# Four blocks' transposes moved from DMA to TensorE, three attention steps and a rescaling placed later, one output buffer fewer

## The chip, the cores and the metric

The kernel runs on one core of a Trainium2 chip. A core has TensorE (PE, matmuls), VectorE (DVE), ScalarE (ACT), GpSimd (POOL) and SyncE (SP), each with its own instruction queue, and 16 DMA engines that all queues share. The metric is the device time of one execution in microseconds (us); the lower the better.

## What is computed

Sliding-window attention with sink tokens, and behind it an RMS norm and a gated feed-forward network (SwiGLU), for 4 sequences of 768 tokens, 8 heads of 64:

```python
scores = scale * np.matmul(q, k.transpose(0, 1, 3, 2))
is_sink = pos[None, :] < n_sink                    # n_sink = 4
in_window = (rel >= 0) & (rel < window)            # window = 128
a = softmax(np.where(is_sink | in_window, scores, -1e9))
x = matmul(a, v)                                   # 3072 tokens x 512
xn = x / sqrt(mean(x * x) + 1e-6) * rms_g
g = xn @ w_gate                                    # 512 -> 1536
out = (g * sigmoid(g) * (xn @ w_val)) @ w_out      # 1536 -> 512
```

## The kernel before

The 3072 tokens are 24 blocks of 128, six to a sequence (`NT`), and four blocks make a group: six groups of 512 tokens (`GB`, `NG`). A block passes through these steps:

- `load_q`, `load_k`, `load_v` (L105 to L124): POOL issues the loads, which convert to bf16. `L.g` in a list of work is all three for block g.
- `T.g` (`a_T`, L298): q and k of a block are transposed into `qkT`, by PE for blocks below `DMA_T_FROM` = 11 and by DMA transposes on SP's queue (L309) from there on.
- `S.g` (`a_S`, L442): scores of block g's keys against its own queries and those of the next block (L455), the exponential on ACT (L465), and the causal masks, on POOL (L431, L436) or DVE (L429).
- `ss` and `a.g`: scores and values of the four sink tokens (L367, L497), for two blocks at a time.
- `v.g.u` (L504): attention times values on PE (L516, L520), reciprocal and norm on DVE (L527, L532); `q.g.u`: the squares for the RMS norm on ACT (L551).
- `y` and `xr.g` (`a_xr`, L610): the root is taken on DVE in a few small steps, and the block is rescaled to `xr` (L622). From block `DMA_X_FROM` = 8 on, SP at once issues a DMA transpose from `xr` into `xnt` (L629); below it, `x.g` (`a_x`, L634) does four PE transposes (L642) and a copy out of PSUM on ACT or DVE (L659).
- The feed-forward network of a group G: gate and value matmuls from `xnt` (L668), tanh on ACT (L682), two products on DVE (L687, L697) into `hT`; then for each of the four blocks 12 output matmuls (L757), a copy times 0.5 on ACT into `osb` (L764), and a store on SP (L770). The very last block is done in two column ranges (`parts_last`, L739 to L746).

What sets the order: up to the middle of group 1 a written list of tokens (`ORDER`, L849) gives the order on every engine. From there on `group(G)` (L887) makes a list of parts, of which a gate or a value matmul set is one, and a third of a block's output matmuls is one. Group 1 has 36 parts: 0 to 23 for gate and value, 24 to 35 for the outputs; the list of tokens covers parts 0 to 11. `run` goes through the parts in order and, ahead of part s, does all work whose slot number is s or less. PE, SP and POOL keep this order; ACT and DVE are arranged by the compiler's scheduler within it.

`step(g, p)` (L820) gives block g's attention work slots from p on: at p the sink scores, `S.g` and the values of block g-1; at p+2 the sink tokens' values where a sequence begins; at p+4 the transposes `T` of block g+3. `AT` (L837) holds p for the four steps of a group, its first row for group 1 (blocks 10 to 13), its second for all later groups. `LOADS` (L885) holds the slots of later loads: in group 1 block 15 at 12.2, 16 at 17.5, 17 at 22.5. The rescaling of the next group's four blocks (`unit_scale`) stands in one slot: 21 in group 1, 22 in group 4, 25 elsewhere (L902). The units `x.g` of the next group have slots 30 to 33 (L904); from block 8 on they hold nothing, since the DMA did it.

Outputs go through the pool `opool` of 4 buffers (L85) of 128x512 in f32; three of them first hold raw inputs at the start (L162). A copy into a buffer waits until the store that last read it has landed. PSUM has 8 banks, which all matmuls share in turn.

Of the kernel before, what the change touches and what calls it, by code (L numbers as in the profile page):

```python
# [11 lines left out]
FP32 = mybir.dt.float32  # L12
# [3 lines left out]
P = 128  # L16
# [12 lines left out]
def kernel(  # L29
# [16 lines left out]
    DM = H * D  # L46
# [17 lines left out]
    RMS_EPS = 1e-6 * RSQRT_SCALE ** 2  # L64
    MS_SCALE = RSQRT_SCALE / math.sqrt(DM)
    DMA_T_FROM = 11
    DMA_X_FROM = 8
    LD = 15
    FA = FTN
    POOL_MASK_FROM = 7  # L70
# [11 lines left out]
    xtpool = ctx.enter_context(tc.tile_pool(name="xtpool", bufs=3))  # L82
    hpool = ctx.enter_context(tc.tile_pool(name="hpool", bufs=FTN // 2))
    spool = ctx.enter_context(tc.tile_pool(name="spool", bufs=3))
    opool = ctx.enter_context(tc.tile_pool(name="opool", bufs=4))  # L85
    psum = ctx.enter_context(
        tc.tile_pool(name="psum", bufs=8, space=bass.MemoryType.PSUM)
    )
# [139 lines left out]
    def bank(name="pT"):  # L228
        return psum.tile([P, 512], FP32, name=name, tag="b1")

    def mover(name, default):
        act = name in ON_ACT or default == "a" and name not in ON_DVE
        return nc.scalar.copy if act else nc.vector.tensor_copy
# [376 lines left out]
    def a_xr(g):  # L610
        def scale():
# [14 lines left out]
            if G not in XNT:  # L626
                XNT[G] = xtpool.tile([P, KTN, GN], BF16, name="xnt")
            if g >= DMA_X_FROM:
                nc.sync.dma_start_transpose(  # L629
# [4 lines left out]
    def a_x(g):  # L634
# [12 lines left out]
        def move():  # L647
# [10 lines left out]
            else:  # L658
                mover(f"x.{g}", "a")(out=dest, in_=src)  # L659
        return [mm, move] if g < DMA_X_FROM else []  # L660

# [66 lines left out]
    def parts_f(G, fts, cols):  # L728

        atoms = ffn_atoms(G, cols, fts)  # L730
        return [lambda: [f() for f in atoms[0:2]], lambda: [f() for f in atoms[2:]]]

    def parts_last(G, tb):

        def cols(c):
            po = bank("po")
            lo, hi = ((0, 3 * P), (3 * P, DM))[c]
            for ft in range(FTN):
                nc.tensor.matmul(  # L739
                    out=po[:, 0:hi - lo], lhsT=HT[(G, ft // 4)][:, ft % 4, tb * P:(tb + 1) * P],  # L740
                    rhs=wo[:, ft, lo:hi], start=(ft == 0), stop=(ft == FTN - 1),
                )
            row = (G * GB + tb) * P
            osb = opool.tile([P, DM], FP32, name="osb")[:, 0:hi - lo]
            nc.scalar.mul(osb, po[:, 0:hi - lo], 0.5)
            (nc.sync, nc.scalar)[c].dma_start(out=out[row:row + P, lo:hi], in_=osb)  # L746

        return [lambda: cols(0), lambda: cols(1)]

    def out_atoms(G, tb):  # L750
        st = {}

        def mm(i):
            if i == 0:
                st["po"] = bank("po")
            for ft in range(4 * i, 4 * i + 4):
                nc.tensor.matmul(  # L757
                    out=st["po"], lhsT=HT[(G, ft // 4)][:, ft % 4, tb * P:(tb + 1) * P],
                    rhs=wo[:, ft, :], start=(ft == 0), stop=(ft == FTN - 1),
                )  # L760

        def move():
            osb = st["osb"] = opool.tile([P, DM], FP32, name="osb")
            nc.scalar.mul(osb, st["po"], 0.5)  # L764

        def store():
            row = (G * GB + tb) * P
            n = P // 2 if G == 4 and tb < 2 else P
            for r in range(0, P, n):
                nc.sync.dma_start(out=out[row + r:row + r + n, :], in_=st["osb"][r:r + n])  # L770

        return [lambda i=i: mm(i) for i in range(FTN // 4)] + [move, store]
# [24 lines left out]
    def unit(name):  # L797
        for f in atoms_of(name):
            f()
# [13 lines left out]
    def unit_scale(gs):  # L813

        with tc.issue_after(LAST[0]):
            unit(f"y.{gs[0]}")
            for g in gs:
                unit(f"xr.{g}")

    def step(g, p):  # L820

        b, t = divmod(g, NT)
        slots = [[] for _ in range(7)]
        if g < NB:
            if t in (2, 4):
                slots[0].append(lambda: unit(f"ss.{b}.{t}.2"))
            slots[0].append(lambda: unit(f"S.{g}"))
            if t == 1:
                slots[2].append(lambda: unit_sink(b))
        if g <= NB:  # L830
            slots[0].append(lambda: unit_attend(g - 1))
        for n in (g + 2, g + 3):
            if n < NB and n not in (10, 11, 12, 13) and by_dma(n) == (n == g + 3):
                slots[4].append(lambda n=n: unit(f"T.{n}"))
        return [(p + i, u) for i, us in enumerate(slots) for u in us]

    AT = [(13, 17, 20, 30), (0, 10, 18, 27)]  # L837

    def run(parts, slots):

# [46 lines left out]
    def group(G):  # L887
        parts, slots = [], []
        for cols in (h0, h1) if G == 1 else (slice(0, GN),):
            n = GN // (cols.stop - cols.start)  # L890
            for ft in range(0, FTN, n):
                parts += parts_f(G, tuple(range(ft, ft + n)), cols)
        g0, n = (10, 4) if G == 1 else (4 * G + 6, 4)
        for g in range(g0, min(g0 + n, NB + 1)):
            slots += step(g, AT[G > 1][g - g0])
        for g, p in LOADS.get(G, {}).items():
            slots.append((p, lambda g=g: unit(f"L.{g}")))
        if G == 1:
            slots.append((12.3, lambda: unit("T.13")))
        if G + 2 <= NG:  # L900
            gs = GROUP[GB * (G + 1)]
            slots.append(({1: 21, 4: 22}.get(G, 25), lambda gs=gs: unit_scale(gs)))  # L902
            for i, g in enumerate(gs):
                slots.append((30 + i, lambda g=g: unit(f"x.{g}")))  # L904
        for tb in range(GB):
            parts += (parts_last if G * GB + tb == NB - 1 else parts_o)(G, tb)
        return parts, slots

    N1 = 12
    with tc.manual_schedule(engines=MANUAL):  # L910
        with tc.manual_schedule(engines=MANUAL_ALL - MANUAL):
            for token in ORDER.split():
                name, i = token.split("/")
                atoms_of(name)[int(i)]()
        parts, slots = group(1)
        run(parts[N1:], [(p - N1, f) for p, f in slots])
        for G in range(2, NG):
            run(*group(G))
# [33 lines left out]
```

## Time and profile before

| | us |
|---|---|
| time, median of 4 runs | 243.9 (243.62 to 245.35) |
| the profiled execution's own time | 244.78 |
| span of the profiled execution, first to last instruction | 243.1 |
| VectorE busy | 164.0 |
| ScalarE busy | 133.6 |
| GpSimd busy | 107.3 |

The profile is of one execution. A busy time is the sum over an engine's instructions; idle time of an engine costs only where another waits for it. A line such as `74.34 0.40 PE L642 MATMUL pxt<-ident,xr x4` reads: from 74.34 us on, for 0.40 us, TensorE ran four matmuls of line 642 that write tile `pxt` from `ident` and `xr`; brackets at the end name the idle time before and what ended it. Matmuls are pipelined, so the next one starts before the end that is shown.

These are the stretches that the text refers to:

| stretch of the span | what runs |
|---|---|
| up to 75.9 us | the written list of tokens |
| 75.9 to 90.2 us | parts 12 to 23 of group 1, with the steps of blocks 10, 11, 12 |
| 90.2 to 102 us | outputs of group 1, with the step of block 13 |
| 103.6 us | first gate matmul of group 2 |
| 127 to 138.5, 163 to 174.6, 198.7 to 209.0 us | outputs of groups 2, 3 and 4 |
| 229.7 to 240.2 us | outputs of group 5 |

### The profile page before, as it was taken

What the parts mean: (1) busy time and instruction counts of PE and PEld (TensorE: products, weight loads), DVE (VectorE), ACT (ScalarE), POOL (GpSimd) and SP (SyncE); (2) the same over time, 40 slices, a digit from 0 to 9 for tenths busy, and PEclk for the clock granted to TensorE, in tenths of its full rate; (3) what the DMA queues carried; (4) which work ended last, traced back from release to release, by engine and by line L of the source; (5) the groups of instructions that cost most, each with busy time, mean ns of one, the idle gap of its engine ahead of it and who ended that gap; (6) DMA issues with size and microseconds to landing.
All of it is one profiled execution on the core that took longest, in us unless ns stands there. A gap on an engine that the chain in (4) does not pass through costs nothing.

```text
span 243.1 us, 5261 instructions
## 1 busy us (share of the span) xinstructions
PE 236.9 (97%) x1991; PEld 137.5 (57%) x2011; DVE 164.0 (67%) x390; ACT 133.6 (55%) x309; POOL 107.3 (44%) x145
## 2 busy tenths in 40 slices
PE   8999999999999999999999999999999999999995
PEld 2578888855877874444444444444444444444443
DVE  5767786894988788067879086869077884287800
ACT  3675738457788873666562567664565342333212
POOL 8966776599549870389992003034032000000000
PEclk9979999999999999999999999999999999999999
DMA  9999999999999996589999666003500003600022
GB/s 128 134 185 185 182 167 199 175 157 176 205 158 112 65 104 71 88 223 153 144 140 101 170 156 89 0 1 42 182 37 3 0 0 69 171 21 1 0 80 96
DMA packets 109291, 26.56 MB, mean 109 GB/s; under 512 B 98385, under 2 KB 106321, under 8 KB 109266
## 3 DMA queue, kind: packets, MB, share of 16 engines
q0 software_dynamic: 80704, 13.90, 78.0%
q1 hardware_dynamic: 27378, 12.00, 24.5%
q10 hardware_dynamic: 1184, 0.33, 0.6%
q8 instruction: 16, 0.26, 0.5%
q14 instruction: 9, 0.07, 0.1%
HBM read 28.31 MB, written 6.29 MB: 142 GB/s over the span
## 4 chain that ended last, share of the span: by engine, by line
PE 92%; DMA 3%; DVE 1%; SPq 1%; issue 1%; ACT 0%; ACTq 0%
PE pg L668 26%; PE pvl L668 26%; PE po L757 22%; PE pT L455 4%; PE pv L516 3%; PE pv L520 3%; PE pqk L237 2%; DMA osb<-in_k_dram 2%; PE po L739 1%; PE pT L386 1%; DMA qkT<-qs 1%; SPq L629 1%; PE pxt L642 1%; PE pv L497 1%; PE pT L401 1%; PE pss L367 1%
## 5 line engine op out<-in xcount | busy, mean ns | idle before, releaser
L668 PE MATMUL pvl<-xnt,wv 128*128 128x512 bf16 (+2 forms) x437 | 74.3, 305 | 0.1
L668 PE MATMUL pg<-xnt,wg 128*128 128x512 bf16 (+2 forms) x432 | 73.4, 304 | 0.9 <-DVE xnt L654 0.3
L687 DVE SCALAR_TENSOR_TENSOR p<-th,pg 128x512 bf16<-128x512 bf16 x72 | 49.2, 684 | 26.1 <-ACT th L682 25.5
L682 ACT ACTIVATE th<-pg 128x512 bf16<-128x512 f32 x72 | 43.1, 601 | 38.4 <-PE pg L668 38.1
L757 PE MATMUL po<-wo,hT 128*128 128x512 bf16 x267 | 61.5, 379 | 0.5
L697 DVE TENSOR_TENSOR hT<-p,pvl 128x512 bf16<-128x512 bf16 x72 | 49.2, 686 | 6.2 <-PE pg L668 0.5
L668 PEld LDWEIGHTS <-wv 128*128 128x128 bf16 x440 | 38.3, 98 | 24.8 <-issue 0.2
L668 PEld LDWEIGHTS <-wg 128*128 128x128 bf16 x440 | 37.5, 98 | 23.2 <-issue 1.3
L431 POOL TENSOR_SCALAR_AFFINE_SELECT et<-et 128x512 bf16<-128x512 bf16 x30 | 20.6, 691 | 65.8 <-ACT et L465 62.6
L757 PEld LDWEIGHTS <-hT 128*128 128x128 bf16 x276 | 26.3, 98 | 29.5
L465 ACT ACTIVATE et<-pT 128x512 bf16<-128x512 f32 x72 | 38.1, 607 | 5.7 <-PE pT L455 5.5
L764 ACT ACTIVATE osb<-po 128x512 f32<-128x512 f32 x23 | 13.7, 594 | 34.2 <-PE po L757 34.2
L551 ACT ACTIVATE sq<-x 128x256 bf16<-128x256 bf16 x42 | 17.6, 423 | 13.5 <-DVE x L532 13.3
L121 POOL DMA_DIRECT2D v<-in_v_dram x24 | 22.0, 916 | 6.3 <-DMA wo<-in_moe_w_out_dram 5.1
L527 DVE RECIPROCAL rden<-pv 128x4 f32<-128x4 f32 x48 | 7.6, 173 | 23.1 <-PE pv L520 23.1
L108 POOL DMA_DIRECT2D qs<-in_q_dram x23 | 21.0, 911 | 2.4 <-issue 1.0
L108 POOL DMA_DIRECT2D ks<-in_k_dram x23 | 20.8, 904 | 1.7 <-DMA wg<-in_moe_w_gate_dram 0.8
L532 DVE TENSOR_TENSOR x<-pv,rden 128x256 bf16<-128x256 f32 x48 | 19.4, 421 | 0.8
L622 DVE SCALAR_TENSOR_TENSOR xr<-x,y,gb 128x512 bf16<-128x512 bf16 x22 | 16.9, 816 | 0.2
L436 POOL TENSOR_SCALAR_AFFINE_SELECT et<-et 128x512 bf16<-128x512 bf16 x24 | 15.8, 660 | 0.0
L520 PE MATMUL pv<-v,et 128*128 128x65 bf16 x160 | 12.4, 194 | 0.0
L455 PE MATMUL pT<-qkT 64*128 64x256 bf16 (+1 forms) x160 | 11.3, 261 | 0.0
(82 smaller groups left out, 184.1 us busy)
## 6 DMA issues: line engine op xcount, KB each, us to landing
out_dram<-osb SPq DMA_DIRECT2D x21, 256.0 KB, 2.3
v<-in_v_dram POOLq DMA_DIRECT2D x24, 128.0 KB, 7.1
qs<-in_q_dram POOLq DMA_DIRECT2D x23, 128.0 KB, 6.8
ks<-in_k_dram POOLq DMA_DIRECT2D x23, 128.0 KB, 6.9
wv<-in_moe_w_val_dram POOLq DMA_DIRECT2D x6, 256.0 KB, 9.0
wg<-in_moe_w_gate_dram POOLq DMA_DIRECT2D x6, 256.0 KB, 8.7
wo<-in_moe_w_out_dram POOLq DMA_DIRECT2D x2, 768.0 KB, 11.1
out_dram<-osb SPq DMA_DIRECT2D x4, 128.0 KB, 3.1
```

Of the source, the lines that this page charges most:

```text
L108: nc.gpsimd.dma_start(out=tl, in_=src[b, :, t * P:(t + 1) * P, :].rearrange("h t d -> t h d"),)
L121: nc.gpsimd.dma_start(out=V16[b][:, t, :, 0:D], in_=v[b, :, t * P:(t + 1) * P, :].rearrange("h t d -> t h d"),)
L431: nc.gpsimd.affine_select(out=ev[:, :, 0, :], in_=ev[:, :, 0, :], compare_op=ALU.is_ge, fill=0.0, base=0, pattern=[[0, x], [1, P]], channe ...
L455: nc.tensor.matmul(out=banks[u][hi][:, j * w:(j + 1) * w], lhsT=QKT[b][pr, 1, hp, t * P:(t + 1) * P], rhs=QKT[b][pr, 0, hp, t * P:t * P + ...
L465: nc.scalar.activation(out=ets[u][:, hi].rearrange("p j n c -> p (j n c)"), in_=banks[u][hi], func=ACT.Exp, scale=inv_sqrt_d,)
L520: nc.tensor.matmul(out=dest, lhsT=E[(g, h, 0)], rhs=V16[b][:, t, h, :], start=(t == 0), stop=True, skip_group_check=True,)
L532: nc.vector.tensor_tensor(out=X16[g][:, heads_of(g, u), :], in0=view()[:, :, 0:D], in1=RDEN.pop((g, u)).unsqueeze(2).to_broadcast((P, 4, D ...
L668: nc.tensor.matmul(out=ps[:, i * w + c0:i * w + c0 + n], lhsT=w_sb[:, kt, ft * P:(ft + 1) * P], rhs=XNT[G][:, kt, cols], start=(kt == 0), ...
L682: LAST_TANH[0] = nc.scalar.activation(out=st["th"], in_=st["pg"], func=ACT.Tanh, scale=0.5).ins
L687: nc.vector.scalar_tensor_tensor(out=st["p1"], in0=st["th"], scalar=1.0, in1=st["pg"], op0=ALU.add, op1=ALU.mult,)
L697: LAST[0] = nc.vector.tensor_tensor(out=HT[key][:, i:i + n, cols], in0=st["p1"].rearrange("p (n c) -> p n c", n=n), in1=st["pvl"].rearrang ...
L757: nc.tensor.matmul(out=st["po"], lhsT=HT[(G, ft // 4)][:, ft % 4, tb * P:(tb + 1) * P], rhs=wo[:, ft, :], start=(ft == 0), stop=(ft == FTN ...
```

## The change

```diff
-    DMA_X_FROM = 8
+    DMA_X_FROM = 12
...
-    opool = ctx.enter_context(tc.tile_pool(name="opool", bufs=4))
+    opool = ctx.enter_context(tc.tile_pool(name="opool", bufs=3))
...
-            osb = opool.tile([P, DM], FP32, name="osb")[:, 0:hi - lo]
+            osb = opool.tile([P, hi - lo], FP32, name=f"ol{c}", bufs=1)
...
-            n = P // 2 if G == 4 and tb < 2 else P
+            n = P // 2 if G == 3 or G == 4 and tb < 2 else P
...
-    AT = [(13, 17, 20, 30), (0, 10, 18, 27)]
+    AT = [(16, 20, 24, 30), (0, 10, 18, 27)]
...
-            slots.append(({1: 21, 4: 22}.get(G, 25), lambda gs=gs: unit_scale(gs)))
+            slots.append(({1: 25, 4: 22}.get(G, 25), lambda gs=gs: unit_scale(gs)))
```

1. Blocks 8 to 11 are transposed by PE: the units `x.8` to `x.11` at slots 30 to 33 of group 1 now hold four PE transposes and a copy on ACT each, and the four DMA transposes on SP go away.
2. In group 1 the steps of blocks 10, 11 and 12 start at parts 16, 20 and 24 instead of 13, 17 and 20, and the transposes `T` of blocks 14 and 15, four slots behind the steps of 11 and 12, move with them. The step of block 13 stays at 30. The loads keep their slots.
3. The rescaling of blocks 8 to 11 stands at slot 25 instead of 21.
4. The output pool has 3 buffers instead of 4; the two pieces of the last block get a buffer of their own each (`ol0`, `ol1`).
5. The four stores of group 3 are issued as two halves of 64 rows each.

On SP's queue the order from group 1 on changes from "transposes of xr 8 to 11; q and k of block 15; three stores; q and k of 16; one store" to "one store; q and k of block 15; two stores; q and k of 16; one store". On POOL's queue the load of block 16 comes ahead of the two masks of block 11 instead of behind them.

## The prediction

> **What bounds the kernel now.** I read the busy times first, then TensorE's gaps in order of time, then the queue of whoever ended a gap, then the stores.
>
> ```profile
> PE 236.9 (97%) x1991; PEld 137.5 (57%) x2011; DVE 164.0 (67%) x390; ACT 133.6 (55%) x309; POOL 107.3 (44%) x145
> PEclk9979999999999999999999999999999999999999
> ```
>
> TensorE (PE) is busy for 236.9 of 243.1 us, at nearly the full granted clock. The other 6.2 us sit mostly at the two ends: by stretches of time, 1.1 us before 6 us, 0.7 us from 6 to 30 us, 2.9 us after 230 us, which the change doesn't touch. What it touches lies between 76 and 104 us (group 1 and the passage to group 2) and at the later passages between groups. So an edit can gain no more than the gaps there, and whatever it adds to PE is paid in full. The one gap is here:
>
> ```profile
> 98.44 3.40 PE L757 MATMUL po<-wo,hT 128*128 128x512 bf16 x15
> 102.31 0.29 PE L367 MATMUL pss<-qkT,ksk 128*32 128x256 bf16 x4 [0.47 <-DMA qkT<-qs]
> 102.53 0.61 PE L455 MATMUL pT<-qkT 64*128 64x256 bf16 x8
> ```
>
> The columns are start, length, engine, line, operation. PE ends group 1's output matmuls at 101.84 us and stands for 0.47 us until the sink scores of blocks 14 and 15 have block 15's transposed q. Why that came late is seen in SyncE's (SP) queue:
>
> ```profile
> 93.52 6.10 SPq L629 DMA_TRANSPOSE xnt<-xr  x4
> 99.71 1.22 SPq L309 DMA_TRANSPOSE qkT<-qs  x1
> 101.03 1.22 SPq L309 DMA_TRANSPOSE qkT<-ks  x1
> 102.34 1.50 SPq L770 DMA_DIRECT2D out_dram<-osb  x3
> ```
>
> The four transposes of xr (blocks 8 to 11, for group 2) stand ahead of block 15's, and three finished outputs wait behind both. The chain of waits says the same: 2.46 us of DMA before the sink scores, behind SP. Most of that passes while PE works on outputs; only 0.47 us of it is PE's loss.
>
> **The change, part by part.**
>
> *xr of blocks 8 to 11 transposed on PE instead of by DMA.* SP loses 4 transposes (6.10 us of its queue). PE gains 16 matmuls with 16 weight loads. The nearest rows are blocks 6 and 7 of the same line:
>
> ```profile
> 74.34 0.40 PE L642 MATMUL pxt<-ident,xr 128*128 128x128 bf16 x4
> 74.57 0.19 PE L516 MATMUL pv<-v,et 128*128 128x65 bf16 x1
> ```
>
> The next operation starts 0.23 us after the first of the four (65.72 to 65.95 us for block 6). Four blocks make 0.92 us. The lower bound is this; the upper is 16 times the mean length of one, 231 ns, unoverlapped: 3.7 us. I take 0.92, since both rows overlap, and 0.03 us a block if the switch to and from the 512-column outputs isn't free: 0.92 to 1.04.
>
> The Trainium skill, page "VectorE: DVE Perf Modes", section "The three transpose paths" and the rules after it, gives 390 ns for a 128x128 transpose on TensorE against 1309 ns by DMA and advises TensorE where PSUM will do. By its figure the sixteen would be an estimated 6.2 us of PE one after another, and the advice would speak for the change; the rows here price what a busy PE pays, which latency doesn't tell.
>
> *The four copies out of PSUM* fall to ScalarE (ACT): 4 of 0.6 us (L659 rows, 585 to 632 ns), 2.4 us. They lie beside PE in the outputs, where ACT's timeline shows it waiting for PE 1.99 us before 95.53 and 1.82 us before 101.88 us. Filling ACT's new order with these durations: exponentials of block 13 until 98.1, squares until 99.1, copies and sink values until 101.3, the third output 101.8, the fourth copy 102.4, the fourth output about 103.4 us. Group 2's first gate matmul needs the fourth copy and the fourth output's bank, at about 104.05 us: 0.65 us of cover. If it were gone, each further us of ACT is a us of PE.
>
> *Attention steps of group 1 at parts 16, 20, 24 instead of 13, 17, 20, and the rescaling at part 25 instead of 21.* No instruction is added. A part is 0.87 us, and the sum of the twelve parts and the steps (14.1 us) fills 75.93 to 90.15 us today, so there is no gap to win by moving, and PE reaches the outputs at 90.15 us either way. What can be lost: block 11's attention is now the last thing before the outputs (about 89.5 to 90.15 us); norm, squares, the seven small steps of the root and four rescalings follow. With VectorE's (DVE) rows: mask and norm of block 11 to 92.65, squares to 93.3, root 1.25, first xr at 95.3, last at 97.3 us. PE needs the first after block 13's scores, at 96.28, and the last at 100.05 us. So it is hidden with 1.0 us to spare. On POOL's queue the load of block 16 (2.75 us) now stands ahead of block 11's masks: masks of block 10 to 83.6, load to 86.3, masks to 87.5 us, needed at 89.5. Block 15's load keeps its place, block 17's stays behind those masks, and neither is needed before 94 us.
>
> *The gap.* On SP block 15's transposes now follow only the first output's store, which waits for ACT at about 93.9 us: q and k issued by 97 and, at the 2.5 us that transposes take to land there, landed by 99.5, against a need at 102.8 us. The 0.47 us is won. Lower bound 0 if it is given back elsewhere; it isn't more than 0.47, since the stall after it would be PE's again.
>
> *Three output buffers instead of four, the last tile's two in buffers of their own.* Each group's fourth output must now wait until the store of its first has landed. Group 1: stored at 94 us, no wait. Group 2: first store is issued at 136.71 us behind four transposes and lands 2.3 us later, 139.0; the fourth output was copied at 138.59 us. ACT starts it 0.4 us late; the exponentials and tanh behind it slip by that, and the PSUM banks that they free are needed 0.7 us later than that or more. Group 3 is tightest, as its stores are also cut in halves:
>
> ```profile
> 166.88 5.31 SPq L629 DMA_TRANSPOSE xnt<-xr  x4
> 172.29 3.34 SPq L770 DMA_DIRECT2D out_dram<-osb  x4
> 174.67 0.60 ACT L764 ACTIVATE osb<-po 128x512 f32<-128x512 f32 x1 [1.99 <-PE po L757]
> ```
>
> ```profile
> out_dram<-osb SPq DMA_DIRECT2D x21, 256.0 KB, 2.3
> out_dram<-osb SPq DMA_DIRECT2D x4, 128.0 KB, 3.1
> ```
>
> The second listing gives KB and us from issue to landing; the four of 128 KB are group 4's halves. These are issued 0.63 us apart from 206.55 us on; the first two landed in 2.3, the later two in 4.1 and 3.9 us. So group 3's second half is issued at 172.92 and lands at 175.2 us; the fourth output is copied 175.25 to 175.85 instead of 174.67 to 175.27. The first gate matmul of group 4 stands at 175.94 us and takes that output's bank: cost 0, with 0.1 us of cover. At 4 us to landing it would be 1.6 us. I take 0 to 0.1. Group 4's fourth output slips from 209.06 to about 209.5 us; only FFN follows, with eight banks ahead: nothing. Eight issues in place of four lengthen SP's queue by 2.5 us, with nothing due behind them before 201 us. The last tile's own buffers move no row: 0.
>
> *Sum.* +0.92 (transposes) +0.06 (switches and group 3) -0.47 (gap) = +0.5 us on the profiled execution's 244.78 us, span 243.1 us, that is 245.3. That execution lies 0.9 us above the median of 243.9 us (243.62 to 245.35); the added work doesn't depend on that, so 243.9 + 0.5 = 244.4 us, +0.2%.
>
> **Rivals.**
>
> *The gap stays (0.12).* The store ahead of block 15's transposes, or ACT's longer order before group 2's first gate, keeps PE standing about 0.5 us. For: that SP transposes have taken up to 2.2 us to issue there (the third of xr at 96.11). Against: 3 us of room by the sum above. 243.9 + 1.0 = 244.9 us. The change would then not do what it says.
>
> *Group 3's fourth output waits for a slow half-store (0.16).* Place: ACT at 174.67 us. It decides once the second half takes longer than 2.4 us to land. Price at the 4.0 us of group 4's later halves: 172.92 + 4.0 + 0.6 - 175.94 = 1.6 us. For: only 0.1 us of cover, and the median of halves is 3.1 us. Against: the two halves issued first landed in 2.3. 244.4 + 1.6 = 246.0 us: slower.
>
> *The rescaling is late (0.06).* PE stands before block 8's transposes at 96.3 us if the first xr comes over 1.0 us later than worked out. In groups 2 and 3 four rescalings took 3.49 instead of 2.74 us, which is 0.2 us for the first; another 1.9 us would have to come from DVE's backlog. At 2 us late: 244.4 + 1.0 = 245.4 us.
>
> *The transposes are free (0.06).* If PE's modelled ends hide slack in the outputs, only the gap counts: 243.9 - 0.5 = 243.4 us. Against: twelve output matmuls fill 2.59 us in the chain, 0.216 us each without a break.
>
> **How the numbers follow.** The forecast of 244.4 us has 0.60. A measurement of this kernel tells about 0.5% (1.2 us) from no change. Within that lie the forecast, the gap that stays, and half of the free transposes and a part of the late rescaling: 0.60 + 0.12 + 0.03 + 0.02 = 0.77. Slower: 0.16 + 0.04 = 0.20. Faster: 0.03. The forecast's own range is 243.9 to 244.9 us (gap won or not, transposes 0.92 to 1.04, medians of a few runs differing by 0.2 us). To leave out no more than 2 in 10 I reach up to the slow half-store and down to the free transposes: 243.4 to 246.1 us.
>
> **What would show it.** Right: 0.23 us for each four transposes at L642 between 96 and 101 us, no gap before L367 near 102.8 us, block 15's transposes on SP before 97 us, the first gate of group 2 about 0.5 us after 103.57 us, and PE's total up by 0.9 us. Wrong: an idle time before PE's gate at about 176 us put down to ACT's output copy; one before L642; or a gate of group 2 that waits for the copied xnt. A time under 243 or over 246.1 us would mean that something outside these steps moved.

## The result, and the profile after

The changed kernel takes 245.34 us (median of 49 runs, 244.47 to 248.44), the kernel before 244.22 us (median of 73 runs, 243.24 to 246.68). The ratio is 1.0047, 95% interval 1.0035 to 1.0058: about 1.1 us longer, just inside the 0.5% that was set as the bound for no change. The profiled execution took 245.34 us with a span of 243.6 us.

The engines' busy times in the page of after:

```profile
PE 237.4 (97%) x2007; PEld 138.1 (57%) x2027; DVE 164.8 (68%) x390; ACT 135.4 (56%) x313; POOL 107.3 (44%) x145
```

TensorE has 16 instructions more, ScalarE four. TensorE's busy time rises by only 0.5 us. Two things blur this total: the profiled execution of before had its granted clock down to 0.59 and 0.56 from 12 to 16 us, and after's had not; and each of the two profiles lacks 20 of TensorE's instructions (1991 and 2007 against 2011 and 2027 in the second profiles of the same kernels, further below). In those second profiles, both with the low clock, it rises from 237.8 to 239.0 us. Totals of one execution each are therefore too coarse for a question of 1 us. What can be compared is the distance between two fixed places in the list of work.

The passage from group 1 to group 2, in TensorE's timeline of after (start, length, engine, line):

```profile
96.16 0.39 PE L642 MATMUL pxt<-ident,xr 128*128 128x128 bf16 x4
96.38 1.03 PE L757 MATMUL po<-wo,hT 128*128 128x512 bf16 x4
...
99.67 0.39 PE L642 MATMUL pxt<-ident,xr 128*128 128x128 bf16 x4
99.90 2.75 PE L757 MATMUL po<-wo,hT 128*128 128x512 bf16 x12
102.58 0.29 PE L367 MATMUL pss<-qkT,ksk 128*32 128x256 bf16 x4
...
103.84 1.02 PE L668 MATMUL pg<-xnt,wg 128*128 128x512 bf16 x3
```

Four transposes hold TensorE from 96.16 to 96.38 us, 0.22 us, and the last four from 99.67 to 99.90. The sink scores at 102.58 us have no bracket: the gap of 0.47 us is gone. SyncE's queue of after shows why:

```profile
93.83 0.34 SPq L770 DMA_DIRECT2D out_dram<-osb  x1
94.25 1.23 SPq L309 DMA_TRANSPOSE qkT<-qs  x1
95.58 1.21 SPq L309 DMA_TRANSPOSE qkT<-ks  x1
```

Block 15's q and k are issued from 94.25 us on instead of 99.71. The last transposes of the written list of tokens in after, and the first gates of groups 2 and 4 in before:

```profile
74.25 0.40 PE L642 MATMUL pxt<-ident,xr 128*128 128x128 bf16 x4
```

```profile
103.57 1.02 PE L668 MATMUL pg<-xnt,wg 128*128 128x512 bf16 x4
...
175.94 1.02 PE L668 MATMUL pg<-xnt,wg 128*128 128x512 bf16 x3
```

From the list's last transposes (L642, 74.34 us before, 74.25 us after) to group 2's first gate (103.57 and 103.84 us) it is 29.23 us before and 29.59 us after: +0.36 us.

The passage from group 3 to group 4, from the timelines of SyncE, ScalarE and TensorE of after:

```profile
167.17 5.56 SPq L629 DMA_TRANSPOSE xnt<-xr  x4
172.82 5.04 SPq L770 DMA_DIRECT2D out_dram<-osb  x8
...
175.90 0.60 ACT L764 ACTIVATE osb<-po 128x512 f32<-128x512 f32 x1 [2.94 <-DMA out_dram<-osb]
...
176.18 0.20 PE L520 MATMUL pv<-v,et 128*128 128x65 bf16 x1
176.54 1.02 PE L668 MATMUL pg<-xnt,wg 128*128 128x512 bf16 x3 [0.17 <-ACT osb L764]
```

This is new. The fourth output's copy on ScalarE, which before waited for TensorE, now waits for a store to land, and behind it TensorE waits for the PSUM bank that the copy frees. Counted from group 2's first gate, group 4's comes after 72.37 us before and 72.70 us after: +0.33 us. The bracket shows 0.17 of it, since it counts from the modelled end of the matmul at 176.18 us, which a gate could have followed 0.03 us after its start. The chain of waits now runs through this place:

```profile
173.43 2.36 DMA out_dram<-osb
175.79 0.02 issue
175.81 0.04 ACTq L764
175.85 0.04 issue
175.90 0.61 ACT osb L764
176.50 0.04 issue
176.54 0.38 PE pg L668
```

From group 4's gate to the last output tile (L739) it is 61.41 us in both. So from the end of the written list on, the traces account for 0.36 + 0.33 = 0.69 us.

### The profile page after: what moved, and what is told of

Its sections match the earlier page's. It is cut to its first block, busy times and chain, and to the rows that moved or that the text cites. A ratio compares the mean times of both kernels' runs of the same rounds, so it can differ in the third digit from the quotient of the medians.

```text
span 243.6 us, 5290 instructions
## 1 busy us (share of the span) xinstructions
PE 237.4 (97%) x2007; PEld 138.1 (57%) x2027; DVE 164.8 (68%) x390; ACT 135.4 (56%) x313; POOL 107.3 (44%) x145
## 4 chain that ended last, share of the span: by engine, by line
PE 87%; DMA 5%; POOL 4%; issue 1%; ACT 1%; DVE 0%; SPq 0%; POOLq 0%; ACTq 0%
PE pvl L668 25%; PE pg L668 25%; PE po L757 23%; DMA wv<-in_moe_w_val_dram 4%; PE pT L455 4%; PE pv L516 2%; PE pv L520 2%; PE pqk L237 1%; PE po L739 1%; POOL v L121 1%; PE pxt L642 1%; DMA out_dram<-osb 1%; POOL wg L141 1%; POOL ks L108 1%; PE pv L497 1%
```

## The experiments

Below, "distance A" is from the written list's last transposes to group 2's first gate, "distance B" from there to group 4's first gate, and "A to end" from the same start to the last output tile. In every profile the stretch from group 4's gate to the last tile was 61.40 or 61.41 us.

Each ratio is to executions of before that were taken beside the kernel (medians 244.13 us for the first four below "after", 244.36 for the next four, 244.21 for the last three), and it is not the quotient of the medians: that would be 1.0037 for "after, whole stores" and 1.0040 for "transposes, steps, rescaling".

| kernel | time, us | ratio to before (95%) | A | B | A to end |
|---|---|---|---|---|---|
| before | 244.22 | 1 | 29.23 | 72.37 | 163.01 |
| after | 245.34 | 1.0047 (1.0035 to 1.0058) | 29.59 | 72.70 | 163.70 |
| transposes on TensorE only | 245.16 | 1.0042 (1.0027 to 1.0057) | 29.59 | 72.37 | 163.37 |
| buffers and halves only | 246.45 | 1.0108 (1.0074 to 1.0141) | 30.43 | 73.10 | 164.93 |
| steps and rescaling only | 247.68 | 1.0136 (1.0096 to 1.0175) | 32.32 | 72.99 | 166.72 |
| block 15 first on SyncE | 243.60 | 0.9985 (0.9965 to 1.0004) | 28.69 | 72.37 | 162.47 |
| after, four buffers | 244.64 | 1.0013 (0.9990 to 1.0037) | 29.59 | 72.37 | 163.36 |
| after, whole stores | 245.26 | 1.0018 (0.9987 to 1.0048) | 29.59 | 72.37 | 163.36 |
| transposes, steps, rescaling | 245.34 | 1.0019 (0.9994 to 1.0045) | 29.59 | 72.37 | 163.36 |
| transposes on TensorE twice | 245.93 | 1.0060 (1.0039 to 1.0081) | 30.49 | 72.37 | 164.26 |
| before, again | 244.23 | 1.0001 (0.9985 to 1.0018) | 29.11 | 72.37 | 162.89 |
| after, again | 245.22 | 1.0043 (1.0026 to 1.0060) | 29.59 | 72.72 | 163.71 |
| block 15 first, again | 244.07 | 0.9991 (0.9977 to 1.0006) | 28.70 | 72.37 | 162.47 |

In these profiles the distances repeat to 0.02 us, except where a wait for a DMA lies in them, or the low clock behind one (steps and rescaling only, B). The times don't: the first 74 us vary, as the last runs show, and so do the waits for a DMA.

### One part of the change at a time

**Transposes on TensorE only.** In the kernel before:

```diff
-    DMA_X_FROM = 8
+    DMA_X_FROM = 12
```

> The kernel before with blocks 8 to 11 transposed on TensorE and nothing else changed. Theory 1 (what the two profiles show: sixteen transposes cost 0.88 us, the gap of 0.47 us before the sink scores goes): +0.4 us, ratio 1.0017, no idle time before L367 near 102 us. Theory 2 (the transposes, with their copies on ScalarE, cost the whole measured difference): +1.1 us, ratio 1.0045.

The time, ratio 1.0042, is the second theory's, and its interval leaves out the first one's 1.0017. Yet the trace shows the gap gone and +0.36 us in distance A, exactly as in after, and nothing more. The time and the distances differ here by about 0.6 us; which of the two is the price of the transposes is settled by the kernel with twice as many of them, below.

**Output buffers and halved stores only.** In the kernel before:

```diff
-    opool = ctx.enter_context(tc.tile_pool(name="opool", bufs=4))
+    opool = ctx.enter_context(tc.tile_pool(name="opool", bufs=3))
...
-            osb = opool.tile([P, DM], FP32, name="osb")[:, 0:hi - lo]
+            osb = opool.tile([P, hi - lo], FP32, name=f"ol{c}", bufs=1)
...
-            n = P // 2 if G == 4 and tb < 2 else P
+            n = P // 2 if G == 3 or G == 4 and tb < 2 else P
```

> The kernel before with three output buffers, own buffers for the last block's two pieces, and halved stores in group 3; transposes, steps and rescaling as before. Theory 1: the fourth output of group 3 waits for the first one's second half to land and TensorE stands 0.2 to 0.4 us before the first gate of group 4: ratio 1.0008 to 1.0017. Theory 2 (buffers cost nothing): 1.000. Theory 3 (in most executions the half lands later than in the profiled one): up to +0.8 us, 1.003.

Slower than every theory had it: 246.45 us. The first two lines are SyncE's queue of this kernel, the others ScalarE and TensorE:

```profile
93.35 5.28 SPq L629 DMA_TRANSPOSE xnt<-xr  x4
...
101.34 1.50 SPq L770 DMA_DIRECT2D out_dram<-osb  x3
...
103.94 0.60 ACT L764 ACTIVATE osb<-po 128x512 f32<-128x512 f32 x1 [4.06 <-DMA out_dram<-osb]
...
104.59 1.02 PE L668 MATMUL pg<-xnt,wg 128*128 128x512 bf16 x4 [1.57 <-ACT osb L764]
```

With the transposes of xr still on SyncE, group 1's first store goes out only at 101.34 us; the fourth output, which needs its buffer, is copied at 103.94 us, and group 2's first gate stands for 1.57 us. Group 4's gate stands 0.56 us, against 0.17 in after: the transposes of xr ahead of group 3's stores took 5.97 us here and 5.56 there, while the second half-store took 2.35 and 2.36 us to land. So it was the later issue that made this stall longer. The parts of the change therefore don't add up one by one: three buffers cost 1.6 us in group 1 with the transposes by DMA, and nothing there once SyncE is free of them.

**Attention steps and rescaling only.** In the kernel before:

```diff
-    AT = [(13, 17, 20, 30), (0, 10, 18, 27)]
+    AT = [(16, 20, 24, 30), (0, 10, 18, 27)]
...
-            slots.append(({1: 21, 4: 22}.get(G, 25), lambda gs=gs: unit_scale(gs)))
+            slots.append(({1: 25, 4: 22}.get(G, 25), lambda gs=gs: unit_scale(gs)))
```

> The kernel before with only the steps at 16, 20, 24 and the rescaling at 25; the transposes stay DMA. Theory 1: moving them adds no work, but xr is ready 1.9 us later (95.3 instead of 93.5 us), so block 15's transposes go out that much later and also behind the first store, and the gap before the sink scores grows from 0.5 to 1.0 to 2.4 us: +0.5 to +1.9 us, ratio 1.002 to 1.008. Theory 2 (the place of steps and rescaling doesn't matter): 1.000 with the gap as before.

The first theory's mechanism, though larger than it said. SyncE's queue and TensorE's timeline of this kernel:

```profile
94.56 5.74 SPq L629 DMA_TRANSPOSE xnt<-xr  x4
100.40 0.53 SPq L770 DMA_DIRECT2D out_dram<-osb  x1
101.02 1.23 SPq L309 DMA_TRANSPOSE qkT<-qs  x1
...
103.57 0.40 PE L367 MATMUL pss<-qkT,ksk 128*32 128x256 bf16 x4 [2.64 <-DMA qkT<-qs]
...
105.75 1.64 PE L668 MATMUL pg<-xnt,wg 128*128 128x512 bf16 x4
```

The later rescaling starts the four DMA transposes later and puts a store ahead of block 15's; the gap grows from 0.47 to 2.64 us, and after it the matmuls are slow (four gate matmuls in 1.64 us to their shown end, instead of 1.02). Distance A grows by 3.1 us. The low clock is likely part of this: of the six executions, two had a mean granted clock of 1.00 and took 246.05 and 246.18 us, 1.9 and 2.05 us above before, at the upper end of the theory's range; four, the profiled one among them, had 0.993 and took 247.57 us or more. Alone, the move is the worst part; it is free only because the transposes leave SyncE.

**Block 15's transposes ahead of xr's on SyncE.** In the kernel before, nothing on TensorE:

```diff
-            if n < NB and n not in (10, 11, 12, 13) and by_dma(n) == (n == g + 3):
+            if n < NB and n not in (10, 11, 12, 13, 14, 15) and by_dma(n) == (n == g + 3):
...
             slots.append((12.3, lambda: unit("T.13")))
+            slots += [(20.5, lambda: unit("T.14")), (20.6, lambda: unit("T.15"))]
```

> The kernel before with block 15's q and k transposes put ahead of the four of xr on SP's queue, nothing else. Theory 1: the gap of 0.47 us goes without any added work: ratio 0.998, sink scores at about 101.85 us. Theory 2: the gap is given back, as the xr transposes land later and the first gate of group 2 waits for xnt instead: 1.000.

SyncE and TensorE of this kernel:

```profile
79.64 1.20 SPq L309 DMA_TRANSPOSE qkT<-qs  x1
81.35 1.19 SPq L309 DMA_TRANSPOSE qkT<-ks  x1
92.81 6.00 SPq L629 DMA_TRANSPOSE xnt<-xr  x4
...
101.06 0.29 PE L367 MATMUL pss<-qkT,ksk 128*32 128x256 bf16 x4
```

The gap is gone by the order on the queue alone, distance A is 0.54 us shorter than before, and the four DMA transposes take their 6.00 us without anyone waiting. This prices the gap of the first profile of before: 0.54 us, won here without work on TensorE.

### What the two stalls and the transposes cost

**After with four buffers, after with whole stores, and the other parts with the old output side.** The first two change one line of after each:

```diff
-    opool = ctx.enter_context(tc.tile_pool(name="opool", bufs=3))
+    opool = ctx.enter_context(tc.tile_pool(name="opool", bufs=4))
```

> The kernel after with four output buffers again, all else as after (halved stores of group 3, buffers of their own for the last tile). Theory 1 (the 0.33 us lost ahead of group 4's first gate is the fourth output copy waiting for the first store's second half, because there are three buffers): with a fourth buffer that copy waits for no store of its own group, no idle time stands before group 4's gate, the first output of group 4 comes 0.33 us sooner relative to group 2's gate (95.3 us after it, as before, instead of 95.6), and the time is after's 245.34 - 0.33 = 245.0 us, ratio to before 1.003. Theory 2 (the halved stores themselves, eight issues on SyncE, delay the group): the idle time before group 4's gate stays and the time stays at 245.3, ratio 1.0047.

```diff
-            n = P // 2 if G == 3 or G == 4 and tb < 2 else P
+            n = P // 2 if G == 4 and tb < 2 else P
```

> The kernel after with group 3's stores whole, three buffers kept. Theory 1 (it is the wait for a store to land, whatever its form): a whole store of 256 KB is issued 0.6 us sooner than a second half and lands in 2.3 us, at about 174.6 us instead of 175.8, so the fourth output is copied before group 4's gate and the 0.17 us idle time before it goes: time 245.0 us, ratio 1.003. Theory 2 (three buffers cost the same with whole stores, since a whole store takes longer to land): the idle time before group 4's gate stays at 0.1 us or more and the time stays at 245.3 us.

In both, distance B is back at 72.37 us. ScalarE's timeline with four buffers:

```profile
174.19 0.60 ACT L764 ACTIVATE osb<-po 128x512 f32<-128x512 f32 x1 [1.99 <-PE po L757]
```

SyncE, ScalarE and TensorE with three buffers and whole stores:

```profile
172.58 3.27 SPq L770 DMA_DIRECT2D out_dram<-osb  x4
...
174.89 0.60 ACT L764 ACTIVATE osb<-po 128x512 f32<-128x512 f32 x1 [2.38 <-DMA out_dram<-osb]
...
175.78 1.02 PE L668 MATMUL pg<-xnt,wg 128*128 128x512 bf16 x3
```

With four buffers the copy waits for TensorE again. With three and whole stores it still waits for the store, issued at 172.58 and landed before 174.89 us, but is over at 175.49, and TensorE doesn't stand, though the transposes ahead took 5.76 us, longer than after's 5.56. So it takes both, three buffers and halves: the second half is issued 0.6 us behind the first and takes as long to land as a whole store. The distances show this. The times say less. With four buffers the interval leaves out the second theory's 1.0047; with whole stores the median of 245.26 us is the second theory's 245.3, and the interval holds both theories' values. Nor do the times tell the two kernels apart.

The third run has the transposes on TensorE, the moved steps and the rescaling at 25, with the output side of before:

> The kernel before with the transposes of blocks 8 to 11 on TensorE, the steps at parts 16, 20, 24 and the rescaling at 25; output buffers and stores as before. Theory 1 (moving the steps and the rescaling costs nothing once SyncE is free of the transposes; only the transposes on TensorE and the output buffers cost): the same as the transposes alone, ratio 1.0042 (1.003 to 1.0055), group 2's first gate 29.6 us after the written list's last transposes, and group 4 without an idle time. Theory 2 (the moved steps have a price of their own, 0.4 us, which is what the profiles leave unexplained): ratio 1.006, that distance 30.0 us.

Distances A and B are those of the transposes alone to 0.01 us. Moving the steps and the rescaling costs nothing once SyncE has no transposes of xr. (The interval of its ratio holds 1.003 and 1.0042 and leaves out the second theory's 1.006; its 30.0 us is excluded by the distance too.)

**The transposes twice over.** In the kernel with the transposes on TensorE only, the sixteen are done a second time into the same place:

```diff
-            for kt in range(KTN):
+            for kt in [*range(KTN)] * (2 if 8 <= g < 12 else 1):
                 nc.tensor.transpose(
```

> The kernel before with the transposes of blocks 8 to 11 on TensorE, each done twice over into the same place (32 instead of 16). The kernel with them once measured 1.0 us above before, where its profile shows only 0.36 us between the written list's end and group 2. Theory 1 (a transpose costs what the profile shows, 0.23 us for four, and the other 0.6 us is a fixed amount that doesn't grow with them): 0.9 us more than with them once, ratio 1.0042 + 0.0038 = 1.008, and group 2's first gate 30.5 us after the written list's last transposes instead of 29.6. Theory 2 (the profile hides part of their price, 1.45 us for sixteen): 1.45 us more, ratio 1.010. Theory 3 (the repeated ones overlap with the output matmuls): under 0.5 us more, ratio below 1.0063.

TensorE's timeline of this kernel:

```profile
95.69 0.61 PE L642 MATMUL pxt<-ident,xr 128*128 128x128 bf16 x8
96.13 0.81 PE L757 MATMUL po<-wo,hT 128*128 128x512 bf16 x3
```

Eight take 0.44 us, and distance A is 30.49 us, 0.90 more than with sixteen. The ratio of 1.0060 is 0.44 us above the single kernel's 1.0042, with wide intervals; its interval excludes the second theory's 1.010, as the distance does, and has the first one's 1.008 at its edge; the third theory has the ratio on its side and is excluded by the distance alone. So the price of a transpose is what the trace shows, 0.90 us for sixteen, twice measured (29.59 less 28.69 of the kernel without the gap, and 30.49 less 29.59). The 0.6 us by which the single kernel's time was longer than its distances is no price of the transposes. An execution of before without its gap would make distance A 0.90 us longer, which the interval of the single kernel's ratio holds; whether that is the reason isn't shown.

The page "TensorE: Matmul & The Clock Gate" of the Trainium skill, section "Wait — 56ns, not 53.3ns?", gives 55.6 ns from start to start for 128-column matmuls at full clock. An estimate from it is 16 x 55.6 ns = 0.89 us, and the runs show 0.90. The 390 ns that the prediction weighed, from another page, is not what a busy TensorE pays.

### The scatter of the first 74 us

**Before, after, and block 15 first, each again**, unchanged, on another chip:

> The kernel before, unchanged, for a second profile. From the written list's last transposes on, the profiles of all kernels so far agree to 0.05 us (163.01 us from there to the last output tile for before, 163.36 with sixteen transposes on TensorE, 164.26 with 32), while the time up to that point varies from 73.4 to 74.5 us between executions of one and the same instruction order. Theory 1 (the part of the difference that the steps don't explain, about 0.45 us, is this scatter of the first 74 us): this profile has 163.0 us again, with the gap before the sink scores of blocks 14 and 15, whatever its first part. Theory 2 (the first profile of before is not typical, and the gap is usually smaller): 162.5 to 162.8 us. Ratio to before 1.000 in both.

> The kernel after, unchanged, for a second profile, beside a second one of before. Theory 1 (steps 0.69 us, the rest scatter of the first 74 us): 163.4 to 163.7 us from the written list's last transposes to the last output tile, depending on how soon group 3's second half-store lands, and a ratio on this chip between 1.002 and 1.0045. Theory 2 (after has a price that its first profile doesn't show): 163.9 us or more, or a first part over 0.3 us longer than that of the profile of before taken beside it, and ratio 1.0047 or more.

> The kernel before with q and k of block 15 transposed ahead of the four transposes of xr on SyncE, a second time on another chip, since the first interval (0.9965 to 1.0004) just reached 1. Theory 1 (the gap of 0.5 us is in nearly every execution of before): ratio 0.998, 162.47 us from the written list's last transposes to the last output tile. Theory 2 (the first measurement was luck of the first 74 us): ratio 1.000.

Before again has 162.89 us from A to end, between the first theory's 163.0 and the second's 162.5 to 162.8, 0.1 us from either: the gap is there again, and smaller. TensorE's timeline, and SyncE's queue:

```profile
102.11 0.29 PE L367 MATMUL pss<-qkT,ksk 128*32 128x256 bf16 x4 [0.34 <-DMA qkT<-qs]
```

```profile
93.44 5.96 SPq L629 DMA_TRANSPOSE xnt<-xr  x4
99.50 1.22 SPq L309 DMA_TRANSPOSE qkT<-qs  x1
```

The four transposes took 5.96 us here and 6.10 the first time, and the gap follows: 0.34 and 0.47. (In the kernel with buffers and halves only they took 5.28 us, and there was no gap.) After again has 163.71 us and a ratio of 1.0043, both as the first theory had them, with the idle time before group 4's gate at 0.18: that stall repeats in its size, the gap of before only in kind. Taken over both pairs, the steps of the change make 0.69 to 0.82 us.

Where the written list ends isn't fixed: its last transposes stood between 73.43 and 74.54 us in thirteen profiles, with the same instructions on TensorE up to there. Four of them (before twice, after the second time, transposes only) show the clock at 0.52 to 0.62 from 12 to 16 us; all four end the list at 74.26 us or later. In the others TensorE waits for first loads here and there: 0.52 us for v at 18.28 us in one, 0.77 for v and 0.20 for a weight in another, none in a third. Block 15 first shows it best: distance A to end 162.47 us both times, the list's end at 73.63 and 74.44, and the spans 241.8 and 242.6 us.

Its two ratios, 0.9985 and 0.9991, lie below 1 with intervals that just reach above it. By distances it is the fastest version, 0.42 to 0.54 us shorter than before and 1.2 us shorter than after; by time it is faster than after, and not told from before.

## Why the prediction came out as it did

The forecast was 244.4 us, slower by less than 0.5%; measured were 245.34 us, slower by 0.47%. The sign and the mechanisms held, and the time lies in the full range, but 0.4 us above the forecast's own range of 243.9 to 244.9. That it lies in the full range is in part luck: the range reached up to 246.1 us for the rival of the slow half-store, while what filled it was a wait of another size, a higher base and a rest that no term of the sum explains. Point by point:

- *Transposes, +0.92 us.* Right: 0.90 us. The switches to and from the outputs cost nothing.
- *The gap, -0.47 us.* Right in kind, and it was won back as described: 0.41 to 0.54 us of distance in the two profiles of before against the kernel without the gap. Distance A grew by 0.36 to 0.48 us; the prediction put group 2's gate at +0.5.
- *Copies on ScalarE, moved steps, rescaling, block 16's load: 0.* Right. The fourth output's copy ran at 102.74 us against 103.4 reckoned for its end (it ended at 103.34); the four xr ran from 94.60 to 97.34 us, against a first at 95.3 and a last at 97.3, and TensorE never stood before L642. Group 2's fourth output waited for its store until 138.98 us and held up nobody; nor did group 4's, which came at 210.23 us instead of the 209.5 reckoned. The kernel with all of these and the old output side is equal to the transposes alone to 0.01 us. What wasn't said is how much of the zero hung on the transposes leaving SyncE: without that, the moved steps cost 3.1 us.
- *Group 3's fourth output, "0 to 0.1".* This is the step that was mis-sized: it cost 0.33 us. The cover was reckoned at 0.1 us with the second half issued at 172.92 us and 2.3 us to landing. Group 2 started 0.27 us later than in before, which moves both sides of that sum alike. But the DMA transposes ahead of the stores took 5.56 us instead of 5.31, so the half was on its way only from 173.43, and it took 2.36 us. These 0.24 and 0.06 us, another 0.06 from landing to copy (0.11 instead of 0.05) and 0.04 from the copy's end to the gate, less the 0.1 of cover, make the 0.3 us. A length that varied from 5.1 to 6.2 us in the same profile was put into the sum as a constant, with 0.1 us of cover behind it.
- *The rival of the slow half-store.* Its place and chain were right, its price was not: 0.33 instead of 1.6 us. "Once the second half takes longer than 2.4 us to land" was the wrong point of decision, since it took 2.36 us and TensorE stood all the same; the time of issue decided it. Group 4's halves had a median of 3.1 us to landing in after too; group 3's eight had 2.3.
- *TensorE's idle time.* Of the 6.2 us that were read as idle, about 1 us is instructions that the profile lacks: the second profile of before has TensorE busy for 237.8 of 242.8 us. Nothing in the sum rests on it.
- *The other rivals.* The gap did not stay, the rescaling was not late, and the transposes were not free.
- *The sum.* By the distances +0.69 to +0.82 us instead of +0.5. Another 0.3 us of the miss is the base: four runs of before had a median of 243.9 us, 73 runs 244.22.
- *What stays open.* The times differ by 1.1 us (0.85 to 1.4 by the interval), the steps explain 0.7 to 0.8 in the profiled executions. The tail behind the last tile is not the rest: it is 5.65 to 5.75 us in the four profiles of before and after. Nor is it the low clock at 12 to 16 us, which shows as a mean of 0.993: beside each other in the last round, the executions of before at 1.00 have medians of 244.03 (16) and 243.92 us (6) and those of after 244.95 (4); at 0.993 it is 244.49 (8) and 244.62 (6), and 245.67 (3). Two places are left. The first 74 us scatter by 1.1 us between executions of the same instructions, so an offset of 0.3 us there can't be told from chance by thirteen profiles, nor be ruled out; no part of the change is at work there that the traces show. And the two waits vary: where four DMA transposes took 5.28 us there was no gap, and where they took 5.97 us ahead of group 3's stores the wait made distance B 0.73 us longer than before's, not 0.33. An execution of before without the gap beside after's profile would make the steps 1.23 us. How often either happens, two profiles of each kernel don't say.

## What to carry to other kernels

Before work is moved from a queue to the engine that sets the time, look whether the order on the queue is enough: here, by the distances, it gained as much (0.4 to 0.5 us) as the move did, without the 0.90 us that the move costs; the times agree but don't prove it. Parts of one change are priced together: three buffers or later steps alone cost 1.6 and 3.1 us in group 1, and nothing there once the queue was free. Where the cover of a wait is smaller than the scatter of what stands ahead of it on its queue, put the cost at the whole scatter and not at zero, and compare kernels by distances between fixed places of the trace when the start varies by more than the change.

## What the runs showed of the hardware

- A half of a store lands hardly sooner than a whole: 12 halves of 128 KB had a median of 2.3 us, the 17 of 256 KB in the same profile 2.4. What a half saves in bytes doesn't show; that it is issued 0.6 us later does.
- After TensorE had stood 2.64 us (steps and rescaling only), its granted clock was 0.60 and 0.75 in the next two stretches; after 1.57 us (buffers and halves only) it stayed at 1.00. By windows, first columns PE, PEld, DVE, ACT, POOL, and the clock third from the end:

```profile
103.00:106.00 3.00, 2.43 (x29) 1.59 (x30) 0.43 (x2) 1.77 (x4) 0.18 (x1) 0.60 0.67 205
106.00:108.00 2.00, 2.00 (x8) 0.80 (x7) 0.69 (x3) 2.00 (x7) 2.00 (x4) 0.75 0.73 152
```

```profile
104.00:106.00 2.00, 1.41 (x7) 0.68 (x7) 0.01 (x1) 2.00 (x5) 0.08 (x1) 1.00 0.87 211
```

The page "TensorE: Matmul & The Clock Gate", section "HAM oscillation — how this bites in real kernels", warns of idle gaps above about 3.4 us. Here a shorter one was followed by the low clock; that the gap caused it is likely from its place, and was seen in one profile only. Two of the six executions of that kernel had a mean granted clock of 1.00, so the drop doesn't come every time.
- Four DMA transposes of the same shape took SyncE 5.28 to 6.10 us to issue, in three profiles with the same instructions up to them (before twice, and the kernel with buffers and halves only, whose outputs have one buffer fewer). The gap before block 15's scores was 0 at 5.28, 0.34 at 5.96 and 0.47 us at 6.10.
